# Other column counts in the second uneven slot, and fewer small stores, in a grouped 1x1 convolution bound by DMA

## The chip, the cores and the metric

One core of one Trainium2 chip. The metric is the device time of one execution in microseconds (us); most comparisons are medians of several executions, and a ratio is given with a 95% interval. A ratio here is the mean time of one kernel's fast runs over that of the other's of the same rounds, so it is not quite the ratio of the medians beside it. The rounds of the experiments ran on four chips, each time beside the kernel before on the same chip; so times are compared within a round, while the profiles of one table come from several chips, one execution of each kernel.

## The reference

A convolution with a 1x1 window and four groups: every pixel has 192 channels, and each group of 48 is multiplied by its own 48x48 matrix. Cut to what matters (k is 1, so there is no padding):

```python
H = W = 512; G = 4; Cg = 48; C = 192
x: (1, 512, 512, 192) bfloat16      w: (1, 1, 4, 48, 48) bfloat16
out = einsum('bhwgc,gcd->bhwgd', x.reshape(B, H, W, G, Cg), w[0, 0]).reshape(B, H, W, C)
```

That is 100.66 MB in and as much out, with little arithmetic: the work is to move the bytes.

## The kernel before

The pixels stand on 128 rows (partitions of SBUF), and a *column* is one pixel of each row: 192 channels of bfloat16, 384 bytes for each row. Loads go through a ring of 240 columns, stores through an output ring of 292. Four columns are a *group* (514 in all). PE (the matrix engine, TensorE) transposes it, VectorE copies the transposed data, PE multiplies, ACT (ScalarE) copies the result into the output ring and issues the stores.

Two blocks of 80 columns, the *slots*, are special: they have no rows 16 to 19, and in the second one other rows may have fewer columns too. What a slot leaves out, the full fields carry.

```python
PARTIAL = (
    ("sync", 0, 16, 4, 0), ("sync", 32, 64, 16, 0),      # queue, first row, rows, outer, columns less
    ("pool", 20, 12, 3, 0), ("pool", 96, 32, 8, 0),
)
UNEVEN = (("sync", 0, 16, 4, 20), *PARTIAL[1:3], ("pool", 96, 32, 8, 2))
FRONT = ((6, PARTIAL), (11, UNEVEN))
# ... (cut)
# plan_stores: where a store ends
if f.full:
    end = min([g for g in OGRID if g > at + 24] or [OCOLS]) - at + c
    # ... (cut)
    if ends and c >= f.cols - LATE_COLS:
        end = min(OCOLS - at, LATE_PART) + c
    end = min([end, f.cols] + [e for e in ends if e > c])
```

ACT waits before it writes over columns of the output ring until the store that read them has landed:

```python
for g in range(NG):
    act.wait_ge(mm_done, g + 1)
    while todo and stores[todo[0]].g1 <= g - 1:
        issue(todo.pop(0))
    if over[g] is not None:
        landed(over[g])          # all semaphores of that store at 16
    act.copy(...)
```

## Time and profile before

The median was 478.08 us of three runs (476.75 to 479.01).

| | before |
|---|---|
| span of the profiled execution | 474.8 us |
| PE / ACT / VectorE busy | 91% / 82% / 52% |
| bytes moved, mean rate | 201.54 MB, 424 GB/s |
| stores, of which late small ones | 34 stores; 44, 44, 28, 32, 16, 12, 8 columns at the end |

To read the page: a busy share is an average over all stages, so the row of 40 slices says more. The row "DMA" there is the mean of the 16 DMA engines of the core. It is full until the end, and yet one engine may be done 3 us before another. What each engine did can be had only from the single transfer records, which the prediction explains. The lines themselves stand in the prediction.

### The profile page before, as it was taken

Reading aid. Unit: us, or ns where it says so; the run is one execution under the profiler, and the core shown is the slowest. Engines: PE = TensorE matmul, PEld = TensorE weight load, DVE = VectorE, ACT = ScalarE, POOL = GpSimd, SP = SyncE. Lnnn points to the kernel's source line nnn. Section 1 sums busy time; section 2 is a strip of 40 time slices with the busy share of each in tenths; the row PEclk is TensorE's granted clock in tenths of the full one; section 3 lists DMA queues with packets and bytes.
Section 4 is the critical chain, followed back from the end, with each engine's and each line's share of the span. In section 5 each row is a group of like instructions: output and inputs, shape, how many; then the busy total and the mean of one; then the engine's idle time right before and its main releaser. Section 6 shows DMA issues by size and latency. Waiting matters only on the chain.

```text
span 474.8 us, 13580 instructions
## 1 busy us (share of the span) xinstructions
PE 431.3 (91%) x6178; PEld 388.6 (82%) x6178; DVE 246.9 (52%) x258; ACT 388.3 (82%) x515; POOL 8.1 (2%) x20
## 2 busy tenths in 40 slices
PE   4999999999998799999998977997998896999992
PEld 3988988888897798888887876986888795988882
DVE  2555555555555455555555543553555552555551
ACT  1889898899997788899897885885988794898884
POOL 1000000000001000000000000000000000000000
PEclk9999999999999999999999998998999997999997
DMA  8999999999999999999999999999999999999997
GB/s 320 425 407 434 427 428 438 431 436 431 429 434 424 435 420 438 438 429 421 436 427 436 433 431 431 430 428 433 431 437 432 436 431 423 438 423 435 427 420 313
DMA packets 9744, 201.54 MB, mean 424 GB/s; under 512 B 1808, under 2 KB 1808, under 8 KB 2448
## 3 DMA queue, kind: packets, MB, share of 16 engines
q1 hardware_dynamic: 4152, 98.00, 48.3%
q10 hardware_dynamic: 4808, 97.99, 48.2%
q0 software_dynamic: 768, 5.36, 2.7%
q8 instruction: 7, 0.11, 0.1%
q14 instruction: 9, 0.07, 0.0%
HBM read 100.68 MB, written 100.66 MB: 424 GB/s over the span
## 4 chain that ended last, share of the span: by engine, by line
PE 63%; DMA 21%; ACT 9%; another core or an unknown queue 3%; issue 1%; ACTq 1%; SPq 0%
PE o_ps L369 37%; PE xT_ps L349 26%; DMA out_dram<-oring 19%; ACT oring L448 9%; DMA ring<-in_x_dram 1%; ACTq L429 1%; SPq L319 0%; SPq L312 0%; ACTq L422 0%; ACTq L431 0%
## 5 line engine op out<-in xcount | busy, mean ns | idle before, releaser
L448 ACT CAST oring<-o_ps 128x768 bf16<-128x768 f32 x514 | 387.0, 801 | 79.7 <-PE o_ps L369 49.4
L411 DVE COPY xT_sb<-xT_ps 128x1536 bf16<-128x1536 bf16 x257 | 246.2, 958 | 215.5 <-PE xT_ps L349 215.5
L369 PE MATMUL o_ps<-wt,xT_sb 128*128 128x144 bf16 (+1 forms) x3084 | 291.0, 237 | 29.4 <-ACT oring L448 24.3
L369 PEld LDWEIGHTS o_ps<-wt,xT_sb 128*128 128x128 bf16 x3084 | 212.7, 99 | 69.5 <-ACT oring L448 59.8
L349 PE MATMUL xT_ps<-ident,ring 128*128 128x128 bf16 x3084 | 220.7, 222 | 4.2 <-DMA ring<-in_x_dram 4.2
L349 PEld LDWEIGHTS xT_ps<-ident,ring 128*128 128x128 bf16 x3084 | 189.0, 99 | 6.7 <-issue 4.6
L296 POOL DMA_DIRECT2D ring<-in_x_dram x4 | 2.2, 558 | 245.5 <-PE xT_ps L349 245.5
L287 POOL DMA_DIRECT2D fill<-in_x_dram x4 | 2.4, 602 | 52.9 <-DMA ring<-in_x_dram 52.9
L306 POOL DMA_DIRECT2D out_dram<-oring x4 | 2.2, 555 | 59.5 <-ACTq L431 59.5
L331 PE MATMUL o_ps<-w_sb,esel 48*128 48x48 bf16 x10 | 0.6, 211 | 2.6 <-DMA w_sb<-in_w_dram 2.6
L331 PEld LDWEIGHTS o_ps<-w_sb,esel 48*128 48x128 bf16 x10 | 0.5, 112 | 2.6 <-POOL esel L274 2.6
L404 DVE CAST wt<-o_ps 128x480 bf16<-128x480 f32 x1 | 0.7, 658 | 3.2 <-PE o_ps L331 3.2
L448 ACT ACT_TABLE_LOAD x1 | 1.3, 1283 | 0.8 <-PEq L468 0.8
L274 POOL TENSOR_SCALAR_AFFINE_SELECT esel<-esel 48x272 bf16<-48x272 bf16 x1 | 0.4, 402 | 0.0
L271 POOL MEMSET esel<- 48x272 bf16 x1 | 0.3, 317 | 0.3 <-POOLq L468 0.3
L278 POOL TENSOR_SCALAR_AFFINE_SELECT ident<-ident 128x128 bf16<-128x128 bf16 x1 | 0.3, 283 | 0.0
L272 POOL MEMSET ident<- 128x128 bf16 x1 | 0.2, 197 | 0.0
L468 POOL MEMSET const-float32-0.0<- 128x1 f32 x1 | 0.1, 98 | 0.3 <-issue 0.3
L468 POOL MEMSET const-bfloat16-1.0<- 128x1 bf16 x1 | 0.1, 101 | 0.0
L468 POOL MEMSET const-uint8-127<- 128x1 uint8 x1 | 0.1, 101 | 0.0
L468 POOL MEMSET const-float32-1.0<- 128x1 f32 x1 | 0.1, 98 | 0.0
## 6 DMA issues: line engine op xcount, KB each, us to landing
ring<-in_x_dram SPq DMA_DIRECT2D x22, 3840.0 KB, 27.6
out_dram<-oring ACTq DMA_DIRECT2D x16, 3456.0 KB, 41.8
out_dram<-oring ACTq DMA_DIRECT2D x5, 3648.0 KB, 43.3
out_dram<-oring ACTq DMA_DIRECT2D x2, 2112.0 KB, 17.1
ring<-in_x_dram SPq DMA_DIRECT2D x2, 1920.0 KB, 25.0
out_dram<-oring ACTq DMA_DIRECT2D x2, 1920.0 KB, 42.9
out_dram<-oring ACTq DMA_DIRECT2D x1, 3072.0 KB, 42.0
out_dram<-oring ACTq DMA_DIRECT2D x1, 2688.0 KB, 45.9
```

The costliest lines, as they stand in the source:

```text
L274: gp.affine_select(out=esel[:], in_=esel[:], pattern=[[-1, ECOLS]], compare_op=AluOpType.is_equal, fill=0.0, base=ESHIFT, channel_multipli ...
L287: gp.dma_start(dst, src).then_inc(fill_sem[k], 16)
L296: gp.dma_start(sbuf, dram).then_inc(ld_sem[ld_key[p.i, n]], 16)
L306: gp.dma_start(dram, sbuf).then_inc(st_sem[i][n], 16)
L331: last = pe.matmul(o_ps[:, NOB - 1, col:col + CG], lhsT=esel[:, s0:s0 + 128], rhs=w_sb[:, g, :], start=True, stop=True, skip_group_check=True)
L349: last = pe.transpose(xT_ps[:, g % NXP, j * 128:(j + 1) * 128], xg[:, j * 128:(j + 1) * 128], ident[:])
L369: last = pe.matmul(o_ps[:, v % NOB, c0_:c1_], lhsT=xs[:, j * 128:(j + 1) * 128], rhs=wt[:, WOFF[tc]:WOFF[tc] + (c1_ - c0_)], start=(tc == ...
L404: dve.tensor_copy(wt[:], o_ps[:, NOB - 1, 0:WCOLS]).then_inc(wc_sem, 1)
L411: dve.tensor_copy(xT_sb[pair % NXS][:, 0:n * 2 * UC].rearrange("p (g c) -> p g c", g=n), xT_ps[:, b0:b0 + n, 0:2 * UC]).then_inc(e_done[pa ...
L429: act.dma_start(dram, sbuf).then_inc(st_sem[i][n], 16)
L448: act.copy(out_columns(g).rearrange("p (u c) -> p u c", u=2), o_ps[:, v % NOB:v % NOB + 2, 0:UC]).then_inc(fa_done[g % (2 * NTOK)] if g < ...
L468: nc = _bacc.Bacc("TRN2", target_bir_lowering=False, num_devices=1)
```

## The change

Its intent: balance the 16 DMA engines better, and send fewer small stores. Rows 0 to 15 get two columns more in the second slot, rows 96 to 127 two more, rows 20 to 31 eight less. The last two stores of the second long field, 72 and 12 columns, become one of 84. Near the end, 44, 44 and 28 columns become 76 and 40.

```diff
-LATE_COLS = 240
+LATE_COLS = 100
-UNEVEN = (("sync", 0, 16, 4, 20), *PARTIAL[1:3], ("pool", 96, 32, 8, 2))
+UNEVEN = (("sync", 0, 16, 4, 18), PARTIAL[1], ("pool", 20, 12, 3, 8), PARTIAL[3])
                 end = min([end, f.cols] + [e for e in ends if e > c])
+                if not ends and f.cols - end < 24 and at + f.cols - c <= OCOLS:
+                    end = f.cols
```

What each engine moves, in columns of a row (384 bytes, once in and once out). The full fields have 1896 columns in both kernels, so 1896 x 8 = 15168 for an engine with eight rows; the first slot adds 640 (engine 4: 320), the second the rest:

| rows of the slot (engine by the formula in the prediction) | before | after |
|---|---|---|
| 0 to 15 (0 to 3) | 16368 | 16376 |
| none (4) | 15808 | 15808 |
| 20 to 31 (5 to 7) | 16448 | 16416 |
| 96 to 127 (8 to 15) | 16440 | 16448 |

## The prediction

> **What bounds the kernel now.** I read the page from the top: busy shares, slices, queues.
>
> ```profile
> span 474.8 us, 13580 instructions
> PE 431.3 (91%) x6178; PEld 388.6 (82%) x6178; DVE 246.9 (52%) x258; ACT 388.3 (82%) x515; POOL 8.1 (2%) x20
> ...
> DMA  8999999999999999999999999999999999999997
> ...
> DMA packets 9744, 201.54 MB, mean 424 GB/s; under 512 B 1808, under 2 KB 1808, under 8 KB 2448
> ...
> q0 software_dynamic: 768, 5.36, 2.7%
> q8 instruction: 7, 0.11, 0.1%
> q14 instruction: 9, 0.07, 0.0%
> ```
>
> The DMA row is full from the second slice to the last but one, so the 16 DMA engines are the bound; PE, at 91%, is close behind. Seven small transfers fetch instructions. They will matter.
>
> Then the end, by the windows view (us; busy time and count of each engine; granted clock, DMA share, GB/s):
>
> ```profile
> 440.00:460.00 20.00, 19.23 (x280) 17.00 (x278) 11.29 (x12) 17.88 (x25) 0.00 (x0) 1.00 1.00 429
> 460.00:470.00 10.00, 6.33 (x88) 5.25 (x85) 3.08 (x4) 7.24 (x10) 0.00 (x0) 0.92 0.98 414
> 470.00:475.00 5.00, 0.00 (x0) 0.00 (x0) 0.00 (x0) 0.00 (x0) 0.00 (x0) 0.50 0.40 163
> ```
>
> DMA share is 1.00 and 0.98 until 470, then 0.40: the engines run out of work at different moments, and the last to finish sets the time. In the timeline the last store is issued at 468.79:
>
> ```profile
> 461.37 0.34 ACTq L429 DMA_DIRECT2D out_dram<-oring  x1
> ...
> 467.58 0.34 ACTq L429 DMA_DIRECT2D out_dram<-oring  x1
> 467.96 0.80 ACT L448 CAST oring<-o_ps 128x768 bf16<-128x768 f32 x1 [0.21 <-issue]
> 468.79 0.34 ACTq L429 DMA_DIRECT2D out_dram<-oring  x1
> ```
>
> Last, the waits of ACT around the second slot; in brackets is the idle time before an entry and what ended it.
>
> ```profile
> 391.05 1.50 ACT L448 CAST oring<-o_ps 128x768 bf16<-128x768 f32 x2 [0.20 <-PE o_ps L369]
> 397.56 0.80 ACT L448 CAST oring<-o_ps 128x768 bf16<-128x768 f32 x1 [5.00 <-DMA out_dram<-oring]
> ```
>
> This 5.00 us is the wait for the store of the 72 columns that the change merges with a small one. It matters for rival two.
>
> **The 16 engines one by one.** The trace's transfer records have no engine number, but a record starts 3 to 4 ns before the one before it on the same engine ends, and the sizes on each queue come in a known order. Chaining the records backwards from the end with these two rules gives 16 chains. From 360 us on no record is left over; of the time before 65 us some are, so I use counts of early records with care. Four chains carry the blocks of rows 0 to 15, three carry 16 records of 30720 bytes from GpSimd's queue (rows 20 to 31), eight carry 8 of 30720 and 8 of 29952 (rows 96 to 127), and one carries none. Their last records end, in us:
>
> - rows 0 to 15: 470.86, 470.87, 472.15, 472.84
> - rows 20 to 31: 471.28, 472.72, 474.01
> - rows 96 to 127: 471.34, 471.41, 471.47, 472.44, 472.52, 472.67, 472.76, 472.77
> - the one without slot rows: 470.87
>
> The stragglers have a cause that the chains show. The eight-chains and three-chains that end near 471.4 hold no instruction fetch; those at 472.4 to 472.8 hold one of 16384 bytes (0.95 us, and some 0.4 us more for the transfer beside it). The one at 474.01 ends 2.7 us after its undisturbed sister, twice such a step; its early part is where records are left over, so two fetches on it is an inference. It alone sets the time; the next engine ends 1.17 us before it.
>
> **What the Trainium skill says.** "DMA: Bandwidth & Descriptors", section "The descriptor swizzle", gives engine = 8 * (partition >> 6) + ((partition >> 2) & 7) for a 128-partition transfer: rows 16 to 19 are engine 4, rows 0 to 15 engines 0 to 3, rows 20 to 31 engines 5 to 7, rows 96 to 127 engines 8 to 15. Section "Why a DMA increments its semaphore by 16 and not by 1" says that a hardware-queue DMA of k parts takes the lowest k engines and a GpSimd one the next k in rotation. The groups of 4, 1, 3 and 8 chains agree. Section "Latency and other measured facts" calls engines 7 and 15 usually slower; here the slow chain is the one without slot rows, hence by the formula engine 4: its 27648-byte stores take 1098 ns (median) against 1025 on the others, its 30720-byte loads 1154 against 1138. The trace differs from the page, and this is why the kernel spares these rows. Section "Queues, rings and completion order" says that an engine alternates between queues packet by packet. The trace agrees: near 390 us the 4608-byte packets of the 12-column store (178 ns) take turns with 30720-byte loads (1138 ns).
>
> **The change, part by part.**
>
> 1. *Columns of the slot.* No engine does less of the full fields. In the second slot each of engines 0 to 3 takes two columns more on four rows, engines 5 to 7 eight columns less on four rows, engines 8 to 15 two more on four rows. A column of a row is 384 bytes, moved in and out, so 768. 30720 bytes take 1134 ns (1138 less the overlap), 27.1 bytes per ns.
>  - engines 5 to 7: 32 x 768 = 24576 bytes less, 0.91 us earlier
>  - engines 0 to 3 and 8 to 15: 8 x 768 = 6144 bytes more, 0.23 us later
>  - engine 4: nothing
>  New ends: 474.01 - 0.91 = 473.10; 472.84 + 0.23 = 473.07; 472.77 + 0.23 = 473.00; engine 4 stays at 470.87. Three groups meet within 0.1 us, which looks like the intent. The end comes 0.9 us earlier, 0.2% of the time. The bytes in all are the same.
>
> 2. *The store of 12 columns is merged into one of 84.* 8 packets less per engine. A 3072-byte record costs 117.6 ns net, a 30720-byte one 1134, so bytes cost 36.8 ns per 1000 and a packet some 5 ns by itself: 0.04 us saved per engine. Not the size, but turn-taking is what changes: a packet of 12 columns gives a load 1138 ns for 178 of its own. The 84-column store (8 packets of 32256 bytes, estimate 1194 ns by that slope) needs 8 x (1194 + 1138) = 18.7 us beside loads, where 72 and 12 took 17.3 + 10.5 = 27.8. Stores gain over loads there for some microseconds; total work does not change.
>
> 3. *Fewer stores near the end.* 44, 44 and 28 columns become 76 and 40; the parts of 32, 16, 12 and 8 stay. That is another 8 packets, 0.04 us. Columns 272 to 316 are now sent with those to 348. Between the stores at 439.12 and 448.21 there are 11 groups, 0.83 us each; the 76-column store is ready 8 groups after 439.12, near 445.7. The earliest engine finishes the store before it at 448.3, so none starves.
>
> 4. *ACT* issues two stores fewer, 0.34 us each on its sequencer. ACT is 82% busy and not the bound: no gain.
>
> Sum: -0.9 us from part 1, -0.1 from parts 2 and 3.
>
> **Rivals.**
>
> First, *the last engine is another one in most executions.* If the two fetches fall on different engines, no engine of rows 20 to 31 stands out; then engines 0 to 3 and 8 to 15, with 0.23 us more, set the time: +0.2 us. For: the three times without a profile spread from 476.75 to 479.01, wider than the whole effect. Against: the fetches follow the same program in each execution. The change doesn't touch the code of PE, though ACT's is four rows shorter.
>
> Second, *the merged store makes ACT wait longer.* ACT at 397.56 waits for the landing of the 72-column store, because it writes over it. Now it waits for 84 columns: 8 x (1194 - 1025) = 1.35 us more, as the wait ends last on engines that alternate with loads. Compute would lag by 1.35 us at most, the last store be issued near 470.1 instead of 468.8. Its first packets start 1.1 us after issue (468.79 to 469.90 before) and eight packets of 3072 take 0.94: an end near 472.2 for the early engines, which is still before 473.1. So it would be hidden, with less than 1 us to spare; a lag of 3 us would cost some 1 us.
>
> Third, *DMA idles somewhere for lack of a ready store.* Two engines already idle by 0.72 and 0.57 us at 461.5 and 467.9, and finish early all the same. For it: the late stores are now larger. Against: parts 32 to 8 and their times are untouched, and part 3's margin is 2.6 us. It would cost up to 1 us.
>
> **Range and chances.** Mechanism: 478.08 - 1.0 = 477.1 if the profiled balance holds; 478.3 if the first rival does; second or third about 478.5 to 479. Weighted by 0.6, 0.25 and 0.15 they give 477.6. With a spread of 2.3 us between three runs, the range is 475.8 to 478.9. Two per cent are 9.6 us, far more than any of these sums: within 2% by 0.975, faster 0.015, slower 0.01.
>
> **What would show it.** Right: the chains of rows 20 to 31 end 0.9 us earlier against the others, the last ends of the three groups lie within 0.5 us, and the last record ends near 473.1 in a fast profile; ACT's wait at the start of that store's space is 5 to 6.5 us; DMA share until 470 stays at 0.98 or above. Wrong: a last engine with rows 0 to 15 or 96 to 127 at 473.5 or later, an idle stretch of several engines after 440 us, or a time below 475 or above 480, which none of these terms explains.

## The result, and the profile after

The changed kernel took 477.03 us (476.12 to 478.91, six runs) against 477.54 (476.75 to 479.01, six runs) before: ratio 0.9989, interval 0.9964 to 1.0013. That is the same time. It lies inside the range.

The page after, the lines that answer to those of before: span, busy time, the DMA row, packets, the GpSimd queue and the instruction fetches.

```profile
span 475.3 us, 13576 instructions
PE 429.1 (90%) x6178; PEld 387.4 (82%) x6178; DVE 246.8 (52%) x258; ACT 388.7 (82%) x515; POOL 8.1 (2%) x20
...
DMA  8999999999999999999999999999999999999997
...
DMA packets 9456, 201.54 MB, mean 424 GB/s; under 512 B 1776, under 2 KB 1776, under 8 KB 2288
...
q0 software_dynamic: 768, 5.34, 2.7%
q8 instruction: 7, 0.11, 0.1%
```

288 packets less, the same bytes at the same mean rate. The end of the changed kernel in the windows view:

```profile
440.00:460.00 20.00, 19.55 (x287) 17.42 (x285) 11.49 (x12) 17.58 (x25) 0.00 (x0) 1.00 1.01 433
460.00:470.00 10.00, 7.49 (x103) 6.21 (x101) 3.83 (x4) 8.38 (x12) 0.00 (x0) 0.98 0.96 406
470.00:475.30 5.30, 0.00 (x0) 0.00 (x0) 0.00 (x0) 0.00 (x0) 0.00 (x0) 0.50 0.59 241
```

PE is busy for 7.49 us of 460 to 470, against 6.33 before: the arithmetic ends later, and the DMA share before 470 has fallen from 0.98 to 0.96. The timeline of ACT in the changed kernel, at the wait after the second slot and at the last stores:

```profile
393.49 1.50 ACT L450 CAST oring<-o_ps 128x768 bf16<-128x768 f32 x2 [0.20 <-PE o_ps L371]
399.54 0.80 ACT L450 CAST oring<-o_ps 128x768 bf16<-128x768 f32 x1 [4.56 <-DMA out_dram<-oring]
...
468.77 0.34 ACTq L431 DMA_DIRECT2D out_dram<-oring  x1
469.15 0.80 ACT L450 CAST oring<-o_ps 128x768 bf16<-128x768 f32 x1 [0.21 <-issue]
469.98 0.35 ACTq L431 DMA_DIRECT2D out_dram<-oring  x1
```

ACT goes on at 399.54 in place of 397.56, and the last store is issued at 469.98 in place of 468.79, 1.2 us later. The wait itself is no longer (4.56 against 5.00), as ACT also came to it later.

The chains of transfer records of the changed kernel, built as the prediction says but allowing for records that overlap (then no record is left over, from the start on, in this and in the profile of before), end at:

- rows 0 to 15: 472.03, 472.06, 473.38, 473.83
- rows 20 to 31: 472.03, 473.30, 473.70
- rows 96 to 127: 472.21, 472.35, 472.42, 473.94, 474.39, 474.40, 474.44, 474.46
- the one without slot rows: 472.07

New is that the last engine is one of rows 96 to 127, 0.6 us after that of any other group. Another thing was overlooked in the prediction: four engines end together at 472.03 to 472.07, 2.1 us after the last store was issued. In the profile before, three do the same at 470.86 and 470.87, 2.1 us after 468.79.

### The profile page after: what moved, and what is told of

Same layout as the page of the kernel before. It is cut to its first block, busy times and chain, and to the rows that moved or that the text cites. A ratio compares the mean times of both kernels' runs of the same rounds, so it can differ in the third digit from the quotient of the medians.

```text
span 475.3 us, 13576 instructions
## 1 busy us (share of the span) xinstructions
PE 429.1 (90%) x6178; PEld 387.4 (82%) x6178; DVE 246.8 (52%) x258; ACT 388.7 (82%) x515; POOL 8.1 (2%) x20
## 4 chain that ended last, share of the span: by engine, by line
PE 55%; DMA 29%; ACT 9%; another core or an unknown queue 4%; issue 1%; ACTq 1%; SPq 0%
PE o_ps L371 32%; PE xT_ps L351 23%; DMA out_dram<-oring 20%; DMA ring<-in_x_dram 9%; ACT oring L450 9%; ACTq L431 1%; SPq L321 0%; SPq L314 0%; ACTq L424 0%; ACTq L433 0%
## 6 DMA issues: line engine op xcount, KB each, us to landing
ring<-in_x_dram SPq DMA_DIRECT2D x2, 1920.0 KB, 27.1
```

## The experiments

**What was asked.** My theory was the prediction's: the engine of rows 20 to 31 that ended last set the time, and the new columns move that end. The main rival: that engine was late by chance, and the last one is usually another. In each profile I read two things from the chains: the mean moment when the engines of a group are done with the store of columns 200 to 272 of the last field (a mark in both kinds of kernel, before most engines begin to wait for stores), and the last end of each group.

Times, each against the kernel before in the same rounds:

| run | columns | 72+12 merged | late stores | median us | ratio (95%) |
|---|---|---|---|---|---|
| before_again | old | no | old | 477.36 | 0.9988 (0.9946 to 1.0031) |
| columns_only | new | no | old | 478.00 | 1.0011 (0.9965 to 1.0058) |
| late_only | old | no | new | 477.24 | 0.9995 (0.9966 to 1.0024) |
| merge_only | old | yes | old | 478.71 | 1.0018 (0.9986 to 1.0050) |
| stores_only | old | yes | new | 476.96 | 0.9983 (0.9944 to 1.0023) |
| after_again | new | yes | new | 477.18 | 1.0009 (0.9974 to 1.0044) |
| relieved | other | yes | new | 477.84 | 1.0012 (0.9983 to 1.0041) |
| balanced | other | no | new | 477.14 | 1.0020 (0.9991 to 1.0049) |
| one_slot | engine 4 spared once | no | old | 481.75 | 1.0084 (1.0034 to 1.0133) |
| one_last_part | new | yes | last 68 in two | 480.00 | 1.0045 (1.0005 to 1.0086) |
| pairs | other, more transfers | yes | new | 493.23 | 1.0343 (1.0304 to 1.0382) |

The kernel before spread from 475.56 to 481.24 over these rounds; no effect of 0.3% can be told from zero by times. What tells the theories apart are the chains:

| profile | mean at the mark: rows 0-15 / 20-31 / 96-127 | 20-31 against 96-127 | last end: rows 0-15 / 20-31 / 96-127 | last store issued |
|---|---|---|---|---|
| before | 449.99 / 451.58 / 451.08 | +0.50 | 472.84 / 474.01 / 472.77 | 468.79 |
| before_again | 449.93 / 452.24 / 452.41 | -0.17 | 473.29 / 474.42 / 475.13 | 470.67 |
| stores_only | 451.08 / 453.04 / 452.89 | +0.15 | 474.20 / 474.72 / 476.61 | 471.93 |
| merge_only | 450.92 / 451.33 / 452.07 | -0.74 | 473.68 / 473.68 / 476.05 | 471.51 |
| late_only | 449.67 / 451.17 / 451.53 | -0.36 | 472.89 / 472.69 / 473.49 | 467.43 |
| columns_only | 450.14 / 450.36 / 451.91 | -1.55 | 473.88 / 472.45 / 475.11 | 470.31 |
| after | 451.53 / 451.87 / 452.53 | -0.66 | 473.83 / 473.70 / 474.46 | 469.98 |
| after_again | 451.86 / 452.03 / 453.05 | -1.02 | 475.20 / 475.13 / 477.99 | 472.98 |
| relieved | 451.93 / 451.36 / 450.66 | +0.70 | 474.82 / 473.03 / 472.25 | 470.05 |

In a few profiles two chains swap partners in mid-run; there I sorted by the packets of the second slot, which come late.

### before_again: the kernel before as its own control

No edit. Expected:

> The kernel before, unchanged, as its own control. Theory (the engine of rows 20 to 31 that ended at 474.01 is last because of what the program gives it): it is last again, about 1.2 us after the engines of rows 96 to 127 that hold a fetch. Rival (it was late by a chance of the start of that one execution): the engines with one fetch, of rows 20 to 31 and of rows 96 to 127, end within 0.5 us of each other, or another is last. Ratio of the times 1.000, with an interval of about 0.002 either way, which is the noise floor for the next two.

Measured: ratio 0.9988, with an interval of 0.004 either way, twice as wide as expected. The last engine is one of rows 96 to 127 at 475.13; the last of rows 20 to 31 ends at 474.42. So the order of the first profile does not hold: the rival is right. The resolved chains also show that the engine that ended at 474.01 in the first profile held one fetch (at 63.2 us), not two; the rest of its delay arose before 16 us, where it was one 30720-byte packet behind its sister without a fetch. In the profiles of two slots in which no chains swap, the seven fetches fall on five engines of rows 96 to 127 and two of rows 20 to 31 every time.

### columns_only: the new columns alone

```diff
-UNEVEN = (("sync", 0, 16, 4, 20), *PARTIAL[1:3], ("pool", 96, 32, 8, 2))
+UNEVEN = (("sync", 0, 16, 4, 18), PARTIAL[1], ("pool", 20, 12, 3, 8), PARTIAL[3])
```

> The new columns in the second slot, the old stores. Theory of the prediction: 0.9 us less than before, ratio 0.998. Rival: the heaviest engine has 16448 columns of rows in both kernels (rows 20 to 31 before, rows 96 to 127 after), so the time is the same, ratio 1.000. In the chains both expect the engines of rows 20 to 31 some 1.1 us earlier against those of rows 96 to 127 than before, comparing engines with one fetch each.

Measured: ratio 1.0011, so no gain is seen, though the interval holds 0.998 too. At the mark the engines of rows 20 to 31 are 1.55 us ahead of those of rows 96 to 127. Over all profiles of the table the old columns give a mean of -0.12 (five, from -0.74 to +0.50) and the new ones -1.08 (three, from -1.55 to -0.66): the columns move these engines, by 1.0 us in the mean where 0.91 + 0.23 = 1.14 was worked out. The ranges touch; relieved, below, confirms it from the other side. But the last engine, 475.11, is one of rows 96 to 127, to which the change gives more.

### stores_only: the new stores alone

```diff
-LATE_COLS = 240
+LATE_COLS = 100
+                if not ends and f.cols - end < 24 and at + f.cols - c <= OCOLS:
+                    end = f.cols
```

> The old columns, the new stores (84 in one, 76 and 40 late). Prediction: 0.1 us less at most, ratio 0.9998. Rival: the merged store makes ACT wait some 1.4 us longer, the last store is issued at 470 instead of 468.8, and the time grows only if this passes the end of the transfers: 0 to 0.5 us more. The store of 84 columns should land about 1 to 2 us after the store of 72 did.

Measured: ratio 0.9983, undecided. In its profile ACT goes on after the second slot at 401.39, and the last store is issued at 471.93; eleven engines end together at 473.99 to 474.20. The profile looks like the longer wait, but it is of the slowest of this kernel's six executions (479.18 us); the times speak for neither.

### one_slot: engine 4 spared in one slot only

```diff
-FRONT = ((6, PARTIAL), (11, UNEVEN))
+FRONT = ((6, (("sync", 0, 16, 4, 12), *PARTIAL[1:])),)
```

> Only the first slot leaves rows 16 to 19 out, so engine 4 has 288 columns of rows more (16096 against 15808), the engines of rows 20 to 31 have 32 less, the rest about the same. Theory (the engine that ends last alone sets the time, and engine 4 is slow): 288 x 768 bytes at the 26.0 bytes per ns that its chain moved before are 8.5 us, so it ends near 479.4 and the time grows by 4 to 6 us, ratio 1.010. Rival (the bytes of all engines together count, the others make up for it): the time is the same within 1 us.

Measured: ratio 1.0084, 481.75 us, 4 us more. The chain of engine 4, which this edit spares in the first slot only, ends at 479.04 (expected 479.4); the next one ends at 473.65. Its windows and its last store, issued at 467.84:

```profile
470.00:480.00 10.00, 0.00 (x0) 0.00 (x0) 0.00 (x0) 0.00 (x0) 0.00 (x0) 0.50 0.21 85
```

```profile
467.84 0.34 ACTq L429 DMA_DIRECT2D out_dram<-oring  x1
```

With the last store long issued, a DMA share of 0.21 over ten microseconds sets the time: one engine of 16. This is the strongest result: one engine alone can set the end, no other helps it, and sparing engine 4 is worth more than anything that this change brought.

### after_again: the changed kernel as its own control

No edit. Expected:

> The changed kernel, unchanged, as its own control. Theory (the heaviest engines are now those of rows 96 to 127, and of these the ones with a fetch and some bad luck end last): the last engine is one of rows 96 to 127, those of rows 20 to 31 reach the store of columns 200 to 272 about 1.1 us ahead of the mean of rows 96 to 127, as in the two runs with the new columns (0.7 and 1.6), where the three runs with the old columns have them 0.2 us behind. Rival (the new columns level the three groups and the last engine is any): an engine of rows 20 to 31 is last. Ratio of the times 0.997 to 1.001.

Measured: ratio 1.0009. Three engines of rows 96 to 127 end at 476.08, 476.95 and 477.99; all other 13 end between 475.04 and 475.26. So the last engine is of that group again. Its ACT timeline after the second slot:

```profile
402.93 0.80 ACT L450 CAST oring<-o_ps 128x768 bf16<-128x768 f32 x1 [10.13 <-DMA out_dram<-oring]
```

A wait of 10.13 us: the store that ACT waits for is landed only when its slowest engine is done. In the chains the engine of median rank ends its part of this store at 391.0, the slowest at 401.06, and ACT goes on 1.9 us after that. So engines that lag delay ACT, and with it the last store (472.98). This profile is of a slow execution, 480.56 us, where the median of the six is 477.18.

### pairs: a failed attempt to tell engines apart

```diff
-UNEVEN = (("sync", 0, 16, 4, 18), PARTIAL[1], ("pool", 20, 12, 3, 8), PARTIAL[3])
+UNEVEN = (("sync", 0, 16, 4, 12), *PARTIAL[1:3], ("pool", 96, 8, 2, 12),
+          ("pool", 104, 8, 2, 8), ("pool", 112, 8, 2, 4), ("pool", 120, 8, 2, 0))
```

> The changed kernel with other columns in the second slot: rows 0 to 15 have 12 less, rows 20 to 31 all, rows 96 to 103, 104 to 111, 112 to 119 and 120 to 127 have 12, 8, 4 and 0 less, each as a transfer of its own over two engines, so that the packet sizes tell these engines apart. Theory: five engines of rows 96 to 127 hold the instruction fetches and it is always the same ones; the sizes show which. If they are the relieved ones, the last of them ends earlier by up to 1.1 us and the engines of rows 0 to 15, with 24 columns of rows or 0.7 us more, or those of rows 20 to 31, with 0.9 us more, become the last: ratio to before 0.996 to 1.001. Rival (the end is a chance of single slow transfers, whichever rows are relieved): the last engine is again one of rows 96 to 127.

Measured: 493.23 us, ratio 1.0343, expected by nobody. The chains could not be resolved (660 records left over), so the question was not answered. The profile shows why it is slow: the timeline of ACT, and the windows.

```profile
418.80 1.50 ACT L451 CAST oring<-o_ps 128x768 bf16<-128x768 f32 x2 [0.20 <-issue]
435.34 1.50 ACT L451 CAST oring<-o_ps 128x768 bf16<-128x768 f32 x2 [15.04 <-DMA out_dram<-oring]
```

```profile
420.00:436.00 16.00, 1.32 (x22) 1.11 (x19) 1.00 (x2) 0.96 (x2) 0.00 (x0) 0.62 1.01 435
436.00:456.00 20.00, 19.50 (x258) 18.09 (x259) 9.58 (x10) 16.40 (x23) 0.00 (x0) 0.87 0.61 259
```

The loads of the GpSimd queue follow one another: the packets of the four new ones begin at 317 to 323, 323 to 333, 333 to 342 and 341 to 348 us, with little overlap. Of the stores two ran side by side (their packets begin at 390.6 to 397.6 and 391.4 to 399.4), the next began at 408.7. With five stores in place of two, the last one landed at 435.24, and ACT, which writes over its columns, stood still for 15.04 us. The DMA engines stayed full for that time and then ran dry, at a share of 0.61. A full DMA row does not mean that a wait costs nothing: it can be paid later.

### one_last_part: the last 68 columns not divided

```diff
-LAST_PARTS = (32, 16, 12, 8)
+LAST_PARTS = (68,)
```

> The changed kernel with its last 68 columns in one store in place of four of 32, 16, 12 and 8. Theory (in all runs so far the engines that are not late have no work left when the last store is issued, and end 2.4 us after its issue together, so the issue of the last store is a floor under the end close below the late engines): 8 packets of 26112 bytes take 7.8 us in place of 8 of 3072 with 0.94, so the floor is 6.8 us higher, and the end comes 4 to 5 us later: ratio 1.009. Rival (the transfers are the bound and a late store only moves work): less than 1 us, ratio 1.002 at most.

The expectation had an error: the output ring ends in the middle, so the 68 columns went out as 32 and 36, and the last store has eight packets of 13824 bytes, some 4.1 us in place of 0.94 (an estimate from 27.1 bytes per ns and 5 ns a packet). Its timeline:

```profile
460.35 0.34 ACTq L431 DMA_DIRECT2D out_dram<-oring  x1
...
467.27 0.34 ACTq L431 DMA_DIRECT2D out_dram<-oring  x1
...
474.00 0.34 ACTq L431 DMA_DIRECT2D out_dram<-oring  x1
```

Fifteen chains end within 0.2 us of each other (479.02 to 479.18), 5.0 us after the last issue, the sixteenth at 480.25. Ratio 1.0045, 2.1 us more (the interval holds 0.2 to 4.1), where the time of the last store grew by 3.2. So the issue of the last store is a floor under the end; the 1 us between the two numbers, as an estimate of the room above the floor, is rough. In the profiles of the table above the floor is 2.1 us after the issue, not the 2.4 of the expectation. The size of the last store matters; for that of the stores before it, which the change altered, no effect was measured.

### merge_only and late_only: the two halves of the store change

merge_only has the two lines with `end = f.cols`, late_only has `LATE_COLS = 100`; both have the old columns.

> The kernel before with only the 72 and 12 columns of the second long field in one store. Theory (the merged store lands later than the 72 columns did, and ACT waits for it): ACT goes on at about 401, as in the two profiles with old columns or new and the new stores (401.4, 402.9 and 399.5), against 397.6, 400.0 and 398.9 with the old ones; the last store is issued at 470.5 to 472.5, 1 to 2 us later than the mean of 469.9 before. Rival (the two groups of profiles differ by chance): ACT goes on at 397.5 to 400, the last store is issued by 470.5. Ratio of the times 0.998 to 1.004 by the first, 0.998 to 1.002 by the second, so the profile, not the time, tells them apart.

> The kernel before with only the late stores changed, 76 and 40 columns in place of 44, 44 and 28. Theory (nothing starves for them, as worked out): ACT goes on after the second slot at 397.5 to 400 as with the old stores, the last store is issued at 468.8 to 470.7, no engine idles at the stores of 76 and 40 columns except the slow one; ratio 0.998 to 1.002. Rival (the larger late stores hold the end up): the last store comes no later, but engines idle by 1 us or more before the store of 76 columns, ratio 1.002 or more.

Measured: ratios 1.0018 and 0.9995. merge_only's profile is divided: ACT goes on at 399.72, which is the rival's range, and the last store is issued at 471.51, the theory's. late_only goes on at 397.18 and issues its last store earliest of all:

```profile
466.60 0.80 ACT L448 CAST oring<-o_ps 128x768 bf16<-128x768 f32 x1 [0.20 <-issue]
467.43 0.38 ACTq L429 DMA_DIRECT2D out_dram<-oring  x1
```

No engine idles before its store of 76 columns. (In stores_only the slow engine did, by 1.8 us at 448.1, and ended with the others.) So no cost of the larger late stores is seen.

For the merged store, five profiles with it (after, after_again, stores_only, merge_only, relieved) have ACT go on at 399.17 to 402.93, mean 400.6, and five without it (before, before_again, columns_only, late_only, balanced) at 397.18 to 399.96, mean 398.6. The last store comes at 471.3 and 469.5 in the mean. That looks like a delay of some 2 us, but the ranges touch, and the profiled executions differ as much: the five with the merged store took 478.56 us in the mean, the five without 477.01, while the medians of the kernels are alike (477.54 and 477.46 in the mean). Among the profiled executions of 477.0 to 477.7 us, the two with it (after, relieved) go on at 399.54 and 399.17, the three without (before_again, columns_only, balanced) at 399.96, 398.89 and 399.24. And the engine of median rank ends the store no later with the merge (391.0 to 394.3) than without (392.3 to 394.5); what is late is a few engines. So a delay by the merge is not shown. In the times nothing of it is seen either: the mean of the ratios is 1.0002 with the merged store (five kernels) and 1.0004 without (four).

### relieved: the columns turned round

```diff
-UNEVEN = (("sync", 0, 16, 4, 18), PARTIAL[1], ("pool", 20, 12, 3, 8), PARTIAL[3])
+UNEVEN = (("sync", 0, 16, 4, 8), *PARTIAL[1:3], ("pool", 96, 32, 8, 8))
```

> The changed kernel with other columns in the second slot: rows 0 to 15 and rows 96 to 127 have 8 less, rows 20 to 31 all. Against the changed kernel the engines of rows 96 to 127 have 32 columns of rows or 0.91 us less, those of rows 0 to 15 have 40 or 1.13 us more, those of rows 20 to 31 have 32 or 0.91 us more. Theory (the engines of rows 96 to 127 end last and these columns shift when an engine is done by what they weigh): those of rows 20 to 31 are done with the store of columns 200 to 272 about 0.7 us behind the mean of those of rows 96 to 127, and not 1.1 us ahead as with the new columns; the last engine can be of any group; ratio 0.997 to 1.001. Rival: the order of the groups does not follow the columns, and the last engine is one of rows 96 to 127 by over 1 us again.

Measured: at the mark the engines of rows 20 to 31 are 0.70 us behind those of rows 96 to 127, as worked out. The eight of rows 96 to 127 all end by 472.26; the last are two of rows 0 to 15, at 474.21 and 474.82, which now have 1.13 us more. So columns shift the groups by their weight. But weight alone does not choose the last engine: rows 20 to 31 are the heaviest here, with 16448 columns against 16416, and end at 473.03. Ratio 1.0012: no gain is seen.

### balanced: what the runs pointed to

No merged store, new late stores, and 13, 4 and 4 columns less for rows 0 to 15, 20 to 31 and 96 to 127.

> What the runs so far point to: no merged store, the late stores of the change, and columns between the changed kernel and the relieved one: in the second slot rows 0 to 15 have 13 less, rows 20 to 31 and rows 96 to 127 have 4 less. Against the changed kernel that is 0.57 us more for the engines of rows 0 to 15, 0.45 us more for rows 20 to 31 and 0.45 us less for rows 96 to 127. Theory: the last ends of the three groups come within 1 us of each other, the last store is issued at 467.4 to 470.7 as with the other kernels without the merged store, and the time is 0 to 1.5 us below before, ratio 0.997 to 1.000. Rival (the end is decided by single slow transfers that differ from execution to execution): the last engine is late by 1 us or more in one group, and the ratio is 1.000 with an interval of 0.003 either way.

Measured: ratio 1.0020 (0.9991 to 1.0049), 477.14 us. The chain profile has rows 0 to 15 end by 473.92 and the other two groups, which have packets of one size here and cannot be told apart, by 474.46: within 1 us, as expected, and no gain is seen. The ends are the theory's, the time is the rival's; and single engines still lag, as two end at 474.39 and 474.46 and the next of their groups at 473.16.

## Why the prediction was right or wrong

- **The range and "within 2%": right.** 477.03 lies in 475.8 to 478.9, and every reason for a gain or a loss was below 1 us by the prediction's own sums. That 477.03 stands next to the 477.1 worked out for the balance is luck: the kernel before, measured beside it, had 477.54 and not 478.08, and the ratio shows no change.
- **Its own signs: most were those of being wrong.** The last engine was one of rows 96 to 127 at 474.46 (named as a sign from 473.5 on); the groups' last ends lay 0.8 us apart, not 0.5; ACT's wait was 4.56 us, not 5 to 6.5; the DMA share before 470 was 0.96, not 0.98.
- **What bounds the kernel: right, but incomplete.** The DMA engines are full. But the last store's issue is a second bound close below. In all nine profiles of the table at least two engines finish together from 2.1 us after the last issue, from two in late_only (469.50 and 469.55 after 467.43) and three in the first profile to thirteen in the changed kernel's control (from 475.04 after 472.98). The prediction gave its early engines such an end, but not as a bound. ACT waits for landings, so this bound moves with the DMA's laggards, the engines that lag behind.
- **Part 1, columns: the shift right, the gain wrong.** Rows 20 to 31 moved by 1.0 us against rows 96 to 127, near the 1.14 worked out, and relieved showed it the other way round. The step that failed is "It alone sets the time", and with it "two fetches on it is an inference". The engine had one fetch and a slow start; in four of five profiles with the old columns and in all three with the new ones the last engine was one of rows 96 to 127, to which the change adds 0.23 us. The table of weights, which needs no trace, gave no reason for a gain: the heaviest engine has 16448 columns of rows in both kernels. The 0.9 us came from one execution's chance.
- **Part 2, the merged store: right in kind, too large in size.** For the median engine the 84-column store took 20.8 us in the changed kernel's profile, and the 72 and 12 columns 27.6 before: the stores gain 6.8 us there, where 9.1 was worked out.
- **Part 3, late stores: right.** Before the 76-column store nothing starved but the slow engine in one profile; no effect on the time was measured (late_only, 0.9995).
- **Part 4, ACT's two issues: right**, in that nothing shows.
- **Rival one (another engine is last): this is what happens.** It had 0.25 of the weight, and deserved most of it. Its reason, fetches that fall differently, was wrong: they fall on the same groups every time.
- **Rival two (ACT waits longer for the merged store): not shown.** The profiles with it have ACT go on some 2 us later, but they are of slower executions, and at equal times the difference is gone.
- **Rival three (idle for lack of a store): wrong for the larger late stores.** The idling that there is comes at the stores after them, with the old late stores too: two engines of rows 0 to 15 wait 2.5 and 2.7 us for the store of 32 columns near 461.5 in before_again, and up to 2.0 us in stores_only. They are not the engines that end last.

One part of the lag goes with the instruction fetches: in before_again and in the changed kernel's profile, where the chains resolve, the five engines of rows 96 to 127 with an instruction fetch are the five of the eight that end last (473.94 to 474.46 against 472.21 to 472.42 in the latter). No run moves the fetches, so that they cause it is not shown. Open: why single engines of rows 96 to 127 fall behind by 2 to 4 us in some executions. Their long packets come mostly after a load has begun anew (near 358, 397 and 401 us) and beside the slot's stores, but no run separates this.

## What to carry to other kernels

When a single engine ends last in one trace, profile the same kernel again before balancing against it, and work out the weights: if the heaviest share is the same before and after, the weights give no reason for a gain. A bound of many parallel engines is set by the slowest one: here a second slot that spares one slow engine (that of rows 16 to 19) was worth 4 us, and evening out the others nothing that could be measured. Look at what the laggards hold up, as ACT goes on only when the last engine of a store is done. And before two profiles are compared, compare the times of the two executions with the medians of their kernels.

## What the Trainium skill lacked or had wrong

- "DMA: Bandwidth & Descriptors", section "Latency and other measured facts", names engines 7 and 15 as the usually slower ones, and ties its guess at the cause to transfers issued from GpSimd, which are 2.7% here. It does not name engine 4. In every resolved profile here the slow engine is the one that serves rows 16 to 19, engine 4 by the page's own formula: 1098 ns for a 27648-byte store against 1025 (medians of the first profile). Given back 288 columns of rows it alone ended at 479.04, and the kernel took 4 us more.
- "Runtime: NRT & Kernel Launch", section "Instruction fetch mechanics", says that instructions come in 16 KiB blocks over a DMA queue of their own and that crossing a block is mostly hidden. The size agrees (7 packets of 16384 bytes), but in a kernel bound by DMA each block takes 0.95 us of one data engine and some 0.4 us of the packet beside it, always on the same two groups of engines.
- No page that I read says that loads of the GpSimd queue to different engines follow one another. In the changed kernel's second slot the packets for rows 20 to 31 begin at 308.6 to 318.3 us and those for rows 96 to 127, on other chains, at 318.1 to 326.5. The stores of the queue do so only in part: in pairs two of five ran side by side, the last landed at 435.24, and ACT stood still for 15.04 us.
